# LSH attention and a gated feed-forward block on one core: query scale folded into the queries, negated maximum as bias, and another order on ScalarE in even slots

## The chip, the cores and the metric

The kernel runs on one core of one Trainium2 chip. The metric is device time in microseconds (us) of one execution. The kernel before takes 633.65 us (median of three runs, 633.51 to 634.42). A difference of 0.2%, some 1.3 us, is about what can be told from none.

The engines are named as in the profile: PE is TensorE's matmuls, PEld its weight loads, DVE is VectorE, ACT is ScalarE, POOL is GpSimd, SP issues DMAs.

## What is computed

There are 4 batches, 8 heads, 768 positions and a head size of 64. Every query and key gets a bucket of 6 sign bits, a query sees only the keys of its own bucket, and the attention's result goes through a gated feed-forward block:

```python
q_bits = (np.einsum('bhsd,dk->bhsk', q, proj) > 0)      # k_bits alike
mask = q_bucket[:, :, :, None] == k_bucket[:, :, None, :]
scores = (1 / np.sqrt(D)) * np.matmul(q, k.transpose(0, 1, 3, 2))
scores = np.where(mask, scores, -1000000000.0)
attn = np.exp(scores - np.max(scores, axis=-1, keepdims=True))
attn = attn / (np.sum(attn, axis=-1, keepdims=True) + 1e-09)
x = np.matmul(attn, v)                                  # heads side by side: B, S, 512
gate = sigmoid(causal 5-tap convolution of x along S, per channel)
out = (gate * (x @ w_val)) @ w_out
```

A query whose bucket holds no key has only masked scores, and its row of `attn` is then 1/768 everywhere. The factor 1/sqrt(D) is 1/8.

## The kernel before

A **unit** is one batch and head (32 of them), a **tile** is 128 queries of a unit against all its 768 keys (6 a unit, 192 in all). The main loop (L453) takes one **slot** k per tile. Every engine runs its instructions in the order in which the program writes them, so the order inside a slot is an order written out by hand.

The mask sits in the matmul: `prep` (L157) stacks, for the unit after the present one, the query rows and twelve rows of bits in `aq`, the key rows and bits in `ak`, and the parts lost by rounding in `bq` and `bk`. A bit that differs adds -2^60 to the score. GpSimd makes `aq` (L166) and `bq` (L168), and SP's DMAs copy the other halves (L169 to L175). `bits` (L186) makes the bit rows of four heads at a time from the raw tiles `r`. The first unit is stacked by `first_prep` (L205) on ACT, DVE and POOL.

What one slot k issues, in this order:

- ACT: `keep_transposed(k-4)`, two copies (L289) that empty the two PSUM banks `tp` into `pt`.
- DVE: `maxima(k)` (L238), the negated row maximum `nm` of the scores; in even slots `row_sums(k-2)` (L262) and `recip(k-2)` (L266) for the pair of tiles k-2 and k-1; `factors(k)` (L244), which is 1/8, or 0 where all scores of a row are masked; and `shifts(k)` (L248), `nm` times that factor.
- POOL: `normalise(k-2)` (L271), in place on `p`.
- PE: `scores(k+1)` (L232), four matmuls into a PSUM buffer `s`.
- ACT: `exponentials(k)` (L256), with `gs` as scale, `nb` as bias and the row sum as accumulator.
- `step(convs)` (in odd slots, from slot 60 on in all): one step of the convolution, on DVE (L323, L332, L334) and POOL (L324).
- Steps that round and split the feed-forward weights (first batch).
- PE and DVE: one step of `moe`, the feed-forward block of the batch before: four matmuls (L365 for the values, L390 for the output) with what follows them; three steps in two slots after the gates (L339, L481).
- `step(preps)`.
- In odd slots: two steps of `attn_v` (L303), two key blocks each; a unit's sixth step also issues the two **value copies** on ACT (L311) from PSUM `av` to `x`.
- PE: `transposes(k-3)` (L280), six matmuls, three into each of the two `tp` banks.

Buffers that matter here: `s` has 2, `tp` 2 (both used by one tile), `av` 1, and the pool of `p` is

```python
pp = ctx.enter_context(tc.tile_pool(name="pp", bufs=LAG + 1))     # line 55, LAG = 3
```

So tile k writes the `p` buffer that tile k-4 used, and its transposes need the banks that the copies of the tile before empty.

Of the kernel before, what the change touches and what calls it, by code (L numbers as in the profile page):

```python
# [19 lines left out]
BIG = float(2.0 ** 60)  # L20
# [6 lines left out]
def kernel(  # L27
# [10 lines left out]
    nc = tc.nc  # L38
    B, H, _, S = qk.shape
# [117 lines left out]
    def prep(i):  # L157

        if i >= len(units):
            return  # L160
        b, h = units[i]
        j = h % 4
        load_values(i)
        r = raws[i]
        aq, ak, bq, bk = stacks[i] = [stk.tile([P, S], FP32R, name=nm) for nm in ("aq", "ak", "bq", "bk")]
        nc.gpsimd.tensor_copy(out=aq, in_=r)  # L166
        yield
        nc.gpsimd.tensor_tensor(out=bq, in0=r, in1=aq.bitcast(FP32), op=ALU.subtract)  # L168
        nc.sync.dma_start(out=ak[0:D].bitcast(FP32), in_=aq[D:P].bitcast(FP32))  # L169
        nc.sync.dma_start(out=bk[0:D].bitcast(FP32), in_=aq[D:P].bitcast(FP32))  # L170
        nc.sync.dma_start(out=bk[D:P].bitcast(FP32), in_=bq[D:P].bitcast(FP32))
        nc.sync.dma_start(out=bq[D:P].bitcast(FP32), in_=aq[0:D].bitcast(FP32))
        u = cur["u"]
        nc.sync.dma_start(out=aq[D:M].bitcast(FP32), in_=u[32 * j:32 * j + 2 * NB].bitcast(FP32))
        nc.sync.dma_start(out=ak[D:M].bitcast(FP32), in_=u[32 * j + 2 * NB:32 * j + 4 * NB].bitcast(FP32))  # L175
        load_raw(i + 5)
        if j == 3 and i + 1 < len(units):
            yield
            yield from bits(i + 1)
# [25 lines left out]
    def first_prep():  # L205

        r = raws[0]
        aq, ak, bq, bk = stacks[0] = [stk.tile([P, S], FP32R, name=nm) for nm in ("aq", "ak", "bq", "bk")]
        z = ps_t.tile([P, 512], FP32, name="tp")
        for g in range(4):  # L210
            nc.tensor.matmul(out=z[32 * g:32 * g + 2 * NB, 0:HS], lhsT=proj_sb[:, 2 * NB * (g // 2):2 * NB * (g // 2 + 1)],
                             rhs=r[:, HS * (g % 2):HS * (g % 2 + 1)], start=True, stop=True, tile_position=(0, 32 * g))
        nc.scalar.copy(out=aq[0:D], in_=r[0:D])
        nc.vector.tensor_copy(out=bk[D:P], in_=r[D:P])
        nc.vector.tensor_copy(out=ak[0:D], in_=r[D:P])
        nc.gpsimd.tensor_tensor(out=bk[0:D], in0=r[D:P], in1=bk[D:P].bitcast(FP32), op=ALU.subtract)
        nc.vector.tensor_tensor(out=bq[D:P], in0=r[0:D], in1=aq[0:D].bitcast(FP32), op=ALU.subtract)
        for g in (0, 2, 3, 1):
            nc.vector.tensor_scalar(out=(aq, ak)[g // 2][D:M, HS * (g % 2):HS * (g % 2 + 1)],
                                    in0=z[32 * g:32 * g + 2 * NB, 0:HS],  # L220
                                    scalar1=rows_sb[32 * g:32 * g + 2 * NB, 2:3],
                                    scalar2=rows_sb[32 * g:32 * g + 2 * NB, 3:4], op0=ALU.is_ge, op1=ALU.mult)
        nc.scalar.copy(out=bq[0:D], in_=r[0:D])

    def scores(k):
        i, qt = tiles[k]
# [7 lines left out]

    def maxima(k):
        s = ss[k]
        nm = small.tile([P, 1], FP32, name="nm")
        nc.vector.tensor_reduce(out=nm, in_=s[:, :, 0:HS], axis=AX.XY, op=ALU.max, negate=True)  # L238
        nms[k] = nm

    def factors(k):

        gs[k] = small.tile([P, 1], FP32, name="gs")
        nc.vector.tensor_scalar(out=gs[k], in0=nms[k], scalar1=BIG / 2, scalar2=scale, op0=ALU.is_lt, op1=ALU.mult)  # L244

    def shifts(k):
        nbs[k] = small.tile([P, 1], FP32, name="nb")
        nc.vector.tensor_scalar(out=nbs[k], in0=nms.pop(k), scalar1=gs[k], scalar2=None, op0=ALU.mult)  # L248

    def exponentials(k):  # L250
        s, nb = ss.pop(k), nbs.pop(k)
        p = pp.tile([P, 2, HS], FP32, name="p")
        if k % 2 == 0:
            cur["sm"] = small.tile([P, 2, 2], FP32, name="sm")
        sm = cur["sm"]
        nc.scalar.activation(out=p, in_=s[:, :, 0:HS], func=AF.Exp, bias=nb, scale=gs.pop(k), accum_out=sm[:, k % 2, 0:1])  # L256
        ps[k] = (p.rearrange("p a b -> p (a b)"), sm)


    def row_sums(k):  # L260
        sums[k] = small.tile([P, 2, 2], FP32, name="s1")
        nc.vector.tensor_scalar(out=sums[k][:, :, 0], in0=ps[k][1][:, :, 0], scalar1=1e-9, scalar2=None, op0=ALU.add)  # L262

    def recip(k):
        ri = small.tile([P, 2], FP32, name="ri")
        nc.vector.reciprocal(out=ri, in_=sums.pop(k)[:, :, 0])  # L266
        rcs[k], rcs[k + 1] = ri[:, 0:1], ri[:, 1:2]

    def normalise(k):
        p, _ = ps[k]  # L270
        nc.gpsimd.tensor_scalar(out=p, in0=p, scalar1=rcs.pop(k), scalar2=1.0, op0=ALU.mult, op1=ALU.mult)  # L271

    def transposes(k):
        p, _ = ps.pop(k)
# [19 lines left out]
    def attn_v(i, pts):  # L294
        b, h = units[i]
        hh, c = h % 2, h // 2
        av = ps_v.tile([P, 512], FP32, name="av")
        vt = vts[i]
        for kb in range(KB):
            if kb:  # L300
                yield
            for s, pt in enumerate(pts):
                nc.tensor.matmul(out=av[s * D:(s + 1) * D, 0:HS], lhsT=vt[:, kb, hh * D:(hh + 1) * D], rhs=pt[kb // 3][:, kb % 3, :],  # L303
                                 start=(kb == 0), stop=(kb == KB - 1), tile_position=(0, s * D))
        if hh == 0:
            x = cur["x"] = xp.tile([P, S + KW - 1], FP32, name="x")
            nc.gpsimd.memset(x[:, 0:KW - 1], 0.0)
        x = cur["x"]
        for s in range(2):
            o = KW - 1 + s * HS  # L310
            nc.scalar.copy(out=x[hh * D:(hh + 1) * D, o:o + HS], in_=av[s * D:(s + 1) * D, 0:HS])  # L311
        if hh == 1:
            if c == 0:
                cur["xs"], cur["g"] = {}, []
            convs.append(pair_x(b, c, x, cur["g"], cur["xs"]))
# [105 lines left out]
    units = [(b, h) for b in range(B) for h in range(H)]  # L421
    tiles = [(i, qt) for i in range(len(units)) for qt in range(KB)]

    raws, stacks, vts, ss, nbs, ps, tps, sums, rcs, nms, gs, cur = {}, {}, {}, {}, {}, {}, {}, {}, {}, {}, {}, {}
    avs, convs, moes = [], [], []
    accs = [(ps_m, "m")]

    def step(gens):
# [13 lines left out]
    with tc.manual_schedule(engines=ENGINES):  # L442
        for i in range(5):
            load_raw(i)
        load_values(0)
        first_prep()
        weights = [[load_conv(), load_weights(0)], [load_weights(1)]]
        preps = [first_bits(), prep(1)]
        scores(0)
        step(weights[0])  # L450
        step(weights[1])
        turn = 0
        for k in range(N + LAG + 1):  # L453
            if 0 <= k - LAG - 1:
                keep_transposed(k - LAG - 1)
            pair = k % 2 == 0 and 0 <= k - 2 < N
            if k < N:
                maxima(k)
            if pair:
                row_sums(k - 2)  # L460
            if k < N:
                factors(k)
            if pair:
                recip(k - 2)
            if 0 <= k - 2 < N:
                normalise(k - 2)
            if k < N:
                shifts(k)
            if k + 1 < N:
                if tiles[k + 1][0] != tiles[k][0]:  # L470
                    finish(preps)
                    preps = [prep(tiles[k + 1][0] + 1)]
                scores(k + 1)
            if k < N:
                exponentials(k)
            if k >= 60 or k % 2:
                step(convs)
# [79 lines left out]
```

## Time and profile before

| | |
|---|---|
| median of the runs | 633.65 us |
| the profiled execution's span | 633.2 us |
| busy share of PE, PEld, DVE, ACT, POOL | 93%, 67%, 71%, 67%, 61% |
| mean granted TensorE clock | 0.986 |
| chain that ended last, by engine | PE 69%, ACT 14%, DVE 12%, issue 2%, DMA 2% |

How to read the views. The page gives each engine's busy time and the chain of waits. The view of the waits has, for each pair of lines, the time that the first sat idle for the second: "us in total, times, longest". The timeline has the start, the length, engine, line, operation, out<-in, shapes, how many were merged, and in brackets the idle time before it with what ended it. The groups by line give busy time, mean nanoseconds of one and the idle time ahead. The view by stage gives, for a stretch "from:to", its length, the busy time of each engine with the number of its instructions behind an x, then the granted clock, the DMA share and GB/s; for one line alone it shows that line's engines only. Matmuls overlap, so their lengths add up to more than the time they take; starts are compared instead.

### The profile page before, as it was taken

The page shows a single profiled execution, that of the slowest core. Times are in us where ns is not written, and L with a number is a line of the kernel's source. Part 1 is how long each engine was busy: PE and PEld are TensorE (multiplying, and loading weights), DVE is VectorE, ACT ScalarE, POOL GpSimd, SP SyncE. Part 2 cuts the span into 40 slices and gives each one's busy share as a digit, 9 for nine tenths or more (in the row PEclk, how much of TensorE's full clock was granted, in tenths as well). Part 3 has the DMA queues.
Part 4 walks back from the last instruction along what each step waited for, and adds up shares of the span by engine and source line. Part 5 has one row for each costly group of instructions (what it writes and reads, how often), then busy time and mean ns, then how long its engine had stood idle before and what let it go on. Part 6 is the DMA issues. An engine that isn't in the chain of part 4 may idle for free.

```text
span 633.2 us, 10639 instructions
## 1 busy us (share of the span) xinstructions
PE 591.4 (93%) x3496; PEld 426.2 (67%) x3496; DVE 451.3 (71%) x1033; ACT 421.1 (67%) x881; POOL 386.0 (61%) x357
## 2 busy tenths in 40 slices
PE   3699888989999999999999999999999999999997
PEld 2476555546667777676657777677667777776895
DVE  5689798999885856668675867668584786665532
ACT  3487777768778676667787776667778667675400
POOL 1476877778966765467754776467663677544221
PEclk9889997989999999999999999999999999999999
DMA  6533534443433334243333234243422223300111
GB/s 244 131 83 92 152 95 139 112 126 91 106 79 80 72 77 122 72 103 97 105 80 93 74 80 122 70 122 81 122 55 61 56 55 81 85 18 2 50 51 50
DMA packets 23270, 56.77 MB, mean 90 GB/s; under 512 B 4296, under 2 KB 4296, under 8 KB 23216
## 3 DMA queue, kind: packets, MB, share of 16 engines
q1 hardware_dynamic: 23072, 56.06, 33.3%
q8 instruction: 28, 0.46, 0.3%
q14 instruction: 26, 0.21, 0.1%
q10 hardware_dynamic: 144, 0.03, 0.0%
HBM read 23.12 MB, written 6.29 MB: 46 GB/s over the span
## 4 chain that ended last, share of the span: by engine, by line
PE 69%; ACT 14%; DVE 12%; issue 2%; DMA 2%; POOL 0%; SPq 0%; ACTq 0%; POOLq 0%; DVEq 0%
PE av L303 19%; PE s L232 17%; PE tp L280 12%; PE m L390 8%; PE m L365 7%; ACT p L256 6%; ACT pt L289 4%; DVE nm L238 3%; ACT x L311 3%; PE tp L365 1%; PE tp L390 1%; PE s L390 1%; DVE u L197 1%; PE tp L194 1%; DVE g L334 1%
## 5 line engine op out<-in xcount | busy, mean ns | idle before, releaser
L271 POOL TENSOR_SCALAR p<-p,ri 128x768 f32<-128x768 f32 x192 | 215.9, 1129 | 173.8 <-DVE nb L248 149.6
L238 DVE TENSOR_REDUCE nm<-s 128x1 f32<-128x768 f32 x192 | 182.5, 951 | 64.3 <-PE s L232 64.2
L289 ACT COPY pt<-tp 128x384 f32<-128x384 f32 x384 | 166.1, 485 | 86.7 <-PE tp L280 85.8
L256 ACT ACTIVATE p<-s,nb,gs 128x768 f32<-128x768 f32 x192 | 192.4, 1002 | 47.0 <-DVE nb L248 41.1
L280 PEld LDWEIGHTS tp<-ident,p 128*128 128x128 f32 x1152 | 131.2, 142 | 73.2 <-issue 46.4
L280 PE MATMUL tp<-ident,p 128*128 128x128 f32 x1152 | 166.3, 281 | 3.8 <-DVE u L197 1.5
L303 PE MATMUL av<-pt,vt 128*64 128x384 f32 x768 | 147.6, 506 | 0.0
L232 PE MATMUL s<-ak,aq 76*128 76x384 f32 x384 | 119.5, 393 | 28.9 <-ACT p L256 24.7
L232 PE MATMUL s<-bk,bq 128*128 128x384 f32 x384 | 101.6, 346 | 0.0
L303 PEld LDWEIGHTS av<-pt,vt 128*64 128x64 f32 x768 | 47.6, 137 | 63.7 <-issue 63.1
L232 PEld LDWEIGHTS s<-ak,aq 76*128 76x128 f32 x384 | 59.9, 196 | 45.2 <-ACT p L256 38.0
L334 DVE SCALAR_TENSOR_TENSOR g<-x,cw_sb,g 128x768 f32<-128x768 f32 x64 | 77.9, 1217 | 0.2
L232 PEld LDWEIGHTS s<-bk,bq 128*128 128x128 f32 x384 | 72.4, 195 | 0.5 <-issue 0.5
L376 POOL TENSOR_TENSOR hl<-ht,hh 128x384 fp32r<-128x384 f32 x32 | 32.2, 1006 | 45.9 <-DVE hh L374 45.9
L168 POOL TENSOR_TENSOR bq<-r,aq 128x768 fp32r<-128x768 f32 x31 | 58.3, 1882 | 0.0
L311 ACT COPY x<-av 64x384 f32<-64x384 f32 x64 | 30.3, 474 | 33.8 <-PE av L303 33.2
L365 PE MATMUL m<-xh,wv 128*128 128x384 f32 x200 | 42.8, 338 | 0.0
L248 DVE TENSOR_SCALAR nb<-nm,gs 128x1 f32<-128x1 f32 x192 | 39.9, 208 | 3.5
L324 POOL TENSOR_TENSOR xl<-x,xh 128x384 fp32r<-128x384 f32 x32 | 33.5, 1062 | 12.3 <-DVE xh L323 12.3
L370 DVE TENSOR_TENSOR ht<-m,g 128x384 f32<-128x384 f32 x25 | 13.9, 555 | 35.4 <-PE m L365 32.0
L256 ACT ACTIVATION_READ_ACCUMULATOR p<-s,nb,gs 128x1 f32 x192 | 39.0, 203 | 0.0
L390 PE MATMUL m<-wo,hh 128*128 128x512 f32 x144 | 38.2, 395 | 0.0
(84 smaller groups left out, 487.4 us busy)
## 6 DMA issues: line engine op xcount, KB each, us to landing
r<-in_qk_dram SPq DMA_DIRECT2D x32, 384.0 KB
vt<-in_v_dram SPq DMA_DIRECT2D x16, 384.0 KB
out_dram<-o SPq DMA_DIRECT2D x24, 256.0 KB
ak<-aq SPq DMA_DIRECT2D x31, 192.0 KB
bk<-aq SPq DMA_DIRECT2D x31, 192.0 KB
bk<-bq SPq DMA_DIRECT2D x31, 192.0 KB
bq<-aq SPq DMA_DIRECT2D x31, 192.0 KB
w<-in_w_val_dram SPq DMA_DIRECT2D x4, 512.0 KB
```

What stands on the lines that cost most here:

```text
L168: nc.gpsimd.tensor_tensor(out=bq, in0=r, in1=aq.bitcast(FP32), op=ALU.subtract)
L232: nc.tensor.matmul(out=s[:, hf, 0:HS], lhsT=lq[0:n, qs], rhs=rk[0:n, hf * HS:(hf + 1) * HS], start=n == M, stop=n == P)
L238: nc.vector.tensor_reduce(out=nm, in_=s[:, :, 0:HS], axis=AX.XY, op=ALU.max, negate=True)
L256: nc.scalar.activation(out=p, in_=s[:, :, 0:HS], func=AF.Exp, bias=nb, scale=gs.pop(k), accum_out=sm[:, k % 2, 0:1])
L271: nc.gpsimd.tensor_scalar(out=p, in0=p, scalar1=rcs.pop(k), scalar2=1.0, op0=ALU.mult, op1=ALU.mult)
L280: nc.tensor.transpose(out=tp[:, n * P:(n + 1) * P], in_=p[:, kb * P:(kb + 1) * P], identity=ident)
L289: nc.scalar.copy(out=pt[:, :, qo:qo + P], in_=tp[:, 0:HS].rearrange("p (a b) -> p a b", b=P))
L303: nc.tensor.matmul(out=av[s * D:(s + 1) * D, 0:HS], lhsT=vt[:, kb, hh * D:(hh + 1) * D], rhs=pt[kb // 3][:, kb % 3, :], start=(kb == 0), s ...
L311: nc.scalar.copy(out=x[hh * D:(hh + 1) * D, o:o + HS], in_=av[s * D:(s + 1) * D, 0:HS])
L334: nc.vector.scalar_tensor_tensor(out=g, in0=x[:, k:k + S], scalar=w, in1=g, op0=ALU.mult, op1=ALU.add)
L365: nc.tensor.matmul(out=acc[:, 0:HS], lhsT=wv[wi][:, c, j * P:(j + 1) * P], rhs=xs_[(c, o)][xi], start=(m == 0), stop=(m == 11))
L390: nc.tensor.matmul(out=acc, lhsT=hs[(o, j)][hi][:, tb * P:(tb + 1) * P], rhs=wo[wi][:, j, :], start=(m == 0), stop=(m == 11))
```

## The change

The diff does four things.

1. The factor 1/8 goes into the queries: for every unit but the first, VectorE multiplies the query half of the raw tile `r` in place, ahead of GpSimd's copy in `prep`; the first unit's copies become scaled copies. `factors` and `shifts` on DVE go, and the exponential has `nm` as its bias and no scale operand.
2. Rows with only masked scores are set right in the normalisation: `evens` makes 1/768 or 0 for a pair of tiles and `factors` turns the reciprocal of the sum into 0 there, so that `normalise` computes p * factor + even. Both work on the pair's two columns, once in two slots.
3. In even slots `exponentials(k)` stands ahead of `keep_transposed(k-4)` on ACT; odd slots keep their order.
4. The value copies are no longer issued with the last step of `attn_v` (odd slots) but in the next even slot, behind the copies of transposes.

The core of it:

```diff
@@ prep
+        nc.vector.tensor_scalar(out=r[0:D], in0=r[0:D], scalar1=scale, scalar2=None, op0=ALU.mult)
         nc.gpsimd.tensor_copy(out=aq, in_=r)
@@ first_prep
-        nc.scalar.copy(out=aq[0:D], in_=r[0:D])
+        nc.scalar.mul(out=aq[0:D], in_=r[0:D], mul=scale)
-        nc.vector.tensor_tensor(out=bq[D:P], in0=r[0:D], in1=aq[0:D].bitcast(FP32), op=ALU.subtract)
+        nc.vector.scalar_tensor_tensor(out=bq[D:P], in0=r[0:D], scalar=scale, in1=aq[0:D].bitcast(FP32),
+                                       op0=ALU.mult, op1=ALU.subtract)
-        nc.scalar.copy(out=bq[0:D], in_=r[0:D])
+        nc.scalar.mul(out=bq[0:D], in_=r[0:D], mul=scale)
@@ maxima, factors and shifts, exponentials
-        nm = small.tile([P, 1], FP32, name="nm")
-        nc.vector.tensor_reduce(out=nm, in_=s[:, :, 0:HS], axis=AX.XY, op=ALU.max, negate=True)
-        nc.vector.tensor_scalar(out=gs[k], in0=nms[k], scalar1=BIG / 2, scalar2=scale, op0=ALU.is_lt, op1=ALU.mult)
-        nc.vector.tensor_scalar(out=nbs[k], in0=nms.pop(k), scalar1=gs[k], scalar2=None, op0=ALU.mult)
+        if k % 2 == 0:
+            cur["nm"] = small.tile([P, 2], FP32, name="nm")
+        nms[k] = cur["nm"][:, k % 2:k % 2 + 1]
+        nc.vector.tensor_reduce(out=nms[k], in_=s[:, :, 0:HS], axis=AX.XY, op=ALU.max, negate=True)
+        if k % 2:
+            pairs[k - 1] = cur["nm"]
-        nc.scalar.activation(out=p, in_=s[:, :, 0:HS], func=AF.Exp, bias=nb, scale=gs.pop(k), accum_out=sm[:, k % 2, 0:1])
+        nc.scalar.activation(out=p, in_=s[:, :, 0:HS], func=AF.Exp, bias=nms.pop(k), accum_out=sm[:, k % 2, 0:1])
@@ evens, factors, normalise
+        nc.vector.tensor_scalar(out=even, in0=pairs[k], scalar1=BIG / 2, scalar2=1.0 / S, op0=ALU.is_ge, op1=ALU.mult)
+        nc.vector.scalar_tensor_tensor(out=ri, in0=pairs.pop(k), scalar=BIG / 2, in1=sums.pop(k + 1),
+                                       op0=ALU.is_lt, op1=ALU.mult)
-        nc.gpsimd.tensor_scalar(out=p, in0=p, scalar1=rcs.pop(k), scalar2=1.0, op0=ALU.mult, op1=ALU.mult)
+        nc.gpsimd.tensor_scalar(out=p, in0=p, scalar1=rcs.pop(k), scalar2=evs.pop(k), op0=ALU.mult, op1=ALU.add)
@@ attn_v
+        outs.append(lambda: values_out(b, hh, c, av))
+
+    def values_out(b, hh, c, av):
@@ the loop over slots
-            if 0 <= k - LAG - 1:
+            if 0 <= k - LAG - 1 and k % 2:
                 keep_transposed(k - LAG - 1)
...
             if pair:
                 row_sums(k - 2)
-            if k < N:
-                factors(k)
-            if pair:
+                evens(k - 2)
                 recip(k - 2)
+                factors(k - 2)
             if 0 <= k - 2 < N:
                 normalise(k - 2)
-            if k < N:
-                shifts(k)
...
             if k < N:
                 exponentials(k)
+            if k % 2 == 0:
+                if 0 <= k - LAG - 1:
+                    keep_transposed(k - LAG - 1)
+                while outs:
+                    outs.pop(0)()
             if k >= 60 or k % 2:
                 step(convs)
```

More of the change, by code (lines that the diff above doesn't have):

```diff
@@ L236, in maxima @@
         s = ss[k]
-        nm = small.tile([P, 1], FP32, name="nm")
[L238 to L248, printed above, removed]
+        if k % 2 == 0:
[4 more added lines that the diff above has]
+            pairs[k - 1] = cur["nm"]
     def exponentials(k):
-        s, nb = ss.pop(k), nbs.pop(k)
+        s = ss.pop(k)
         p = pp.tile([P, 2, HS], FP32, name="p")
@@ L255, in exponentials, with evens, factors @@
         sm = cur["sm"]
-        nc.scalar.activation(out=p, in_=s[:, :, 0:HS], func=AF.Exp, bias=nb, scale=gs.pop(k), accum_out=sm[:, k % 2, 0:1])
+        nc.scalar.activation(out=p, in_=s[:, :, 0:HS], func=AF.Exp, bias=nms.pop(k), accum_out=sm[:, k % 2, 0:1])
         ps[k] = (p.rearrange("p a b -> p (a b)"), sm)
     def row_sums(k):
-        sums[k] = small.tile([P, 2, 2], FP32, name="s1")
-        nc.vector.tensor_scalar(out=sums[k][:, :, 0], in0=ps[k][1][:, :, 0], scalar1=1e-9, scalar2=None, op0=ALU.add)
+        sums[k] = small.tile([P, 2], FP32, name="s1")
+        nc.vector.tensor_scalar(out=sums[k], in0=ps[k][1][:, :, 0], scalar1=1e-9, scalar2=None, op0=ALU.add)
+    def evens(k):
+        even = small.tile([P, 2], FP32, name="ev")
+        nc.vector.tensor_scalar(out=even, in0=pairs[k], scalar1=BIG / 2, scalar2=1.0 / S, op0=ALU.is_ge, op1=ALU.mult)
+        evs[k], evs[k + 1] = even[:, 0:1], even[:, 1:2]
     def recip(k):
+        r0 = sums[k + 1] = small.tile([P, 2], FP32, name="r0")
+        nc.vector.reciprocal(out=r0, in_=sums.pop(k))
+    def factors(k):
         ri = small.tile([P, 2], FP32, name="ri")
-        nc.vector.reciprocal(out=ri, in_=sums.pop(k)[:, :, 0])
+        nc.vector.scalar_tensor_tensor(out=ri, in0=pairs.pop(k), scalar=BIG / 2, in1=sums.pop(k + 1),
+                                       op0=ALU.is_lt, op1=ALU.mult)
         rcs[k], rcs[k + 1] = ri[:, 0:1], ri[:, 1:2]
@@ L422 @@
     tiles = [(i, qt) for i in range(len(units)) for qt in range(KB)]
-    raws, stacks, vts, ss, nbs, ps, tps, sums, rcs, nms, gs, cur = {}, {}, {}, {}, {}, {}, {}, {}, {}, {}, {}, {}
-    avs, convs, moes = [], [], []
+    raws, stacks, vts, ss, ps, tps, sums, rcs, evs, nms, pairs, cur = {}, {}, {}, {}, {}, {}, {}, {}, {}, {}, {}, {}
+    avs, outs, convs, moes = [], [], [], []
     accs = [(ps_m, "m")]
@@ L491 @@
         finish(avs)
+        while outs:
+            outs.pop(0)()
         cur["gates"] = 0
```

## The prediction, made before the result

> **What bounds the kernel now.** I read the page first, then the waits by engine, then the timeline of one stretch engine by engine, then the stages.
>
> ```profile
> span 633.2 us, 10639 instructions
> PE 591.4 (93%) x3496; PEld 426.2 (67%) x3496; DVE 451.3 (71%) x1033; ACT 421.1 (67%) x881; POOL 386.0 (61%) x357
> ```
>
> ```profile
> PE s L232 <- ACT p L256: 24.7, 40, 3.4
> ```
>
> TensorE is busy 93% of the span, and what it waits for is one thing: the scores (L232) wait 40 times, 24.7 us in all, for an exponential (L256) that must give a PSUM score buffer back. So I looked at what makes that exponential late. These are rows of the matmul timeline, then of ScalarE's, then of VectorE's, in a stretch without feed-forward work (start, length, what):
>
> ```profile
> 301.88 0.61 PE L232 MATMUL s<-ak,aq 76*128 76x384 f32 x2 [0.25 <-ACT p L256]
> ...
> 304.22 0.88 PE L280 MATMUL tp<-ident,p 128*128 128x128 f32 x6
> 304.85 0.60 PE L232 MATMUL s<-ak,aq 76*128 76x384 f32 x2
> ...
> 305.65 0.82 PE L280 MATMUL tp<-ident,p 128*128 128x128 f32 x6
> 306.70 0.62 PE L232 MATMUL s<-ak,aq 76*128 76x384 f32 x2 [0.23 <-ACT p L256]
> ...
> 309.04 0.87 PE L280 MATMUL tp<-ident,p 128*128 128x128 f32 x6
> ...
> 312.04 0.62 PE L232 MATMUL s<-ak,aq 76*128 76x384 f32 x2 [0.42 <-ACT p L256]
> ```
>
> ```profile
> 304.81 0.86 ACT L289 COPY pt<-tp 128x384 f32<-128x384 f32 x2 [1.21 <-PE tp L280]
> 305.55 1.01 ACT L256 ACTIVATE p<-s,nb,gs 128x768 f32<-128x768 f32 x1
> ...
> 306.53 0.87 ACT L289 COPY pt<-tp 128x384 f32<-128x384 f32 x2
> ...
> 309.15 0.97 ACT L311 COPY x<-av 64x384 f32<-64x384 f32 x2 [0.73 <-PE av L303]
> ```
>
> ```profile
> 302.89 0.96 DVE L238 TENSOR_REDUCE nm<-s 128x1 f32<-128x768 f32 x1 [0.47 <-PE s L232]
> ...
> 309.66 0.92 DVE L323 CAST xh<-x 128x384 fp32r<-128x384 f32 x2 [0.54 <-ACT x L311]
> 310.66 0.96 DVE L238 TENSOR_REDUCE nm<-s 128x1 f32<-128x768 f32 x1
> ```
>
> Call an even slot k. Its maximum is there at 303.85, but ScalarE idles 1.21 us, because first in its queue are the copies of the transposes of tile k-4, and those transposes start only at 304.22. The copies start at 304.81 (after the third transpose), the exponential at 305.55, and the scores of k+2 at 306.70. I measure everything from the first transpose of tile k-4: scores of k+2 come **2.48 us** later (306.70 - 304.22). Every third even slot has the value copies in front too, and there it is **3.00 us** (312.04 - 309.04).
>
> **What the new order makes of that ring.** The exponential may not simply start at 303.85. It writes a p buffer; line 55 gives LAG+1 = 4 of them, so tile k takes the one of tile k-4, whose last readers are the six transposes at 304.22 to 305.10. Today this wait is invisible, since the copies in front of the exponential wait for the same transposes, but for the third instead of the sixth. So the exponential gains only 305.55 - 305.14 = 0.41 us. The copies, now behind it, lose more; and the next transposes (tile k-3, same slot) need both of the two tp PSUM banks that these copies empty. The new ring from the first transpose:
>
> - 0.88 until the sixth transpose has ended (row 304.22), and 0.04 to the start that this allows (an estimate, at most the 0.14 by which the scores of 306.70 follow the exponential's end at 306.56);
> - 0.90 from the exponential's start to the next copy: 0.98 today (305.55 to 306.53), less one pointer operand;
> - 0.86 for the two copies, 0.03 release;
> - 0.32 for the three transposes into the second bank: six take 304.85 - 304.22 = 0.63;
> - then the scores of k+2. Sum **3.03 us**.
>
> The exponential's own saving has these rows:
>
> ```profile
> L256 ACT ACTIVATE p<-s,nb,gs 128x768 f32<-128x768 f32 x192 | 192.4, 1002 | 47.0 <-DVE nb L248 41.1 <-DVE cwt L92 4.1 <-PE tp L280 1.2
> ...
> L248 DVE TENSOR_SCALAR nb<-nm,gs 128x1 f32<-128x1 f32 x192 | 39.9, 208 | 3.5
> ...
> L244 DVE TENSOR_SCALAR gs<-nm 128x1 f32<-128x1 f32 x192 | 29.2, 152 | 3.3
> ...
> L338 ACT ACTIVATE g<-g 128x768 f32<-128x768 f32 x16 | 12.2, 832 | 0.0
> ```
>
> With two pointer operands it takes 1.00 us, the sigmoid of the same size with none 0.83. Dropping one of two lies between 0 and 0.17; I take half, 0.08. If it is 0, the ring is 3.11; if 0.17, 2.94.
>
> So each even slot costs the larger of 3.03 and what it has today. Where feed-forward matmuls stand between the scores and the transposes, today's figure is larger:
>
> ```profile
> 215.14 0.88 PE L280 MATMUL tp<-ident,p 128*128 128x128 f32 x6
> ...
> 217.82 0.59 PE L232 MATMUL s<-ak,aq 76*128 76x384 f32 x2
> ```
>
> ```profile
> 233.04 0.87 PE L280 MATMUL tp<-ident,p 128*128 128x128 f32 x6
> ...
> 235.95 0.59 PE L232 MATMUL s<-ak,aq 76*128 76x384 f32 x2
> ```
>
> That is 2.68 with a step of four value matmuls (L365) and 2.91 with one of four output matmuls (L390). The losses per even slot: plain 0.55, with value copies 0.03, with L365 0.35, with L390 0.12.
>
> **How many of each.** The views by stage, first of the maxima (L238), then of L365, then of L390; the number behind x counts instructions:
>
> ```profile
> 38.00:190.00 152.00, 52.39 (x56) 0.97 0.42 110
> 300.00:327.00 27.00, 9.56 (x10) 1.00 0.39 100
> 457.00:472.00 15.00, 5.29 (x6) 1.00 0.30 73
> ```
>
> ```profile
> 190.00:578.00 388.00, 120.83 (x127) 1.00 0.32 81
> ```
>
> ```profile
> 190.00:578.00 388.00, 60.96 (x286) 50.62 (x287) 1.00 0.32 81
> ```
>
> ```profile
> 190.00:578.00 388.00, 47.68 (x180) 33.31 (x180) 1.00 0.32 81
> ```
>
> Two slots are a pair. Without feed-forward work there are 28 pairs in the first batch (38 to 190 us) and 5 + 3 = 8 in two later gaps. The other 127 - 16 = 111 slots are 55 pairs with it, a third of them (18) with value copies. L365 has 286/4 = 71 steps, of which 12 share a slot with two others (the gates counter, lines 339 and 481: 3 batches, 2 slots, 2 extra steps), so 59 slots; L390 has 45. Half of each are even, two thirds of those without value copies: 20 and 15.
>
> - The 8 pairs: today a pair lasts 306.70 - 301.88 = 4.82, with value copies 5.34, mean 4.99; in the new order 4.82 + 0.55 = 5.37 for all. 8 x 0.38 = **+3.0**.
> - The 55 pairs: 20 x 0.35 + 15 x 0.12 + 18 x 0.03 = **+9.3**.
> - The 28 pairs of the first batch. Here VectorE is the other limit:
>
> ```profile
> 38.00:190.00 152.00, 137.88 (x830) 89.62 (x831) 134.53 (x300) 114.77 (x250) 117.39 (x104) 0.97 0.42 110
> ```
>
> A pair takes 152/28 = 5.43, that is 0.44 over the ring's 4.99, because VectorE (134.53/28 = 4.80 of work a pair) is 96% of that ring and its maxima come late. The change takes two gs and two nb off a pair (0.72) and puts two ops of two columns in (between 0.15 and 0.21 each, so 0.36), and a third of a query scaling (below, 0.2). VectorE is then at 4.64 of 5.37, 86%. The lateness falls to between 0 and 0.44; I take 0.2: 28 x (5.57 - 5.43) = **+4** (from -2 to +11).
>
> **The other edits.** The query scaling is a VectorE op ahead of GpSimd's copy of the same unit (31 times). A row of its kind stands alone at 0.61 and beside a GpSimd op at 1.75:
>
> ```profile
> 314.37 0.61 DVE L332 TENSOR_SCALAR g<-x,cw_sb 128x768 f32<-128x768 f32 x1
> ```
>
> ```profile
> 80.43 1.75 DVE L332 TENSOR_SCALAR g<-x,cw_sb 128x768 f32<-128x768 f32 x1
> ```
>
> I take 0.6, since GpSimd's next op, the copy, waits for it; behind that copy waits a normalisation whose factor VectorE makes later still, so the wait costs nothing there. The Trainium skill, "GPSIMD Engine Reference", section 1 Specifications, says that GpSimd shares its SBUF interfaces with VectorE and contends with 2-port ops: by it, and by the second row, the first batch would pay up to 9 x 1.15 = 10 us more VectorE time, which I keep for the upper end. The unit's DMAs on SP's queue start later by the same 0.6 us, for a unit that begins six slots (three pairs of some 5 us) later; only at the start is there no such cover:
>
> ```profile
> 20.31 0.67 DVE L197 TENSOR_SCALAR u<-m,packed 128x384 fp32r<-128x384 f32 x1
> ```
>
> ```profile
> 20.32 0.82 POOL L166 CAST aq<-r 128x768 fp32r<-128x768 f32 x1
> ```
>
> Unit 1's copy would start at 20.98 + 0.6 instead of 20.32, +1.26, less one gs and one nb (0.36) on the way there, and through GpSimd's subtraction and two DMAs it sets when tile 6 begins: **+0.7** (0 to 1.9). First-unit edits replace copies with scaled copies of the same size: 0. The normalisation gets a second pointer operand on GpSimd; even at the 0.17 above, 192 of them are 33 us of the 247 that GpSimd is idle: 0.
>
> The value copies move behind the copies of transposes. From slot 60 on, the split of x (L323) is queued in the same slot on VectorE, ahead of the odd slot's maximum. It would wait from 309.66 to about 312.7 (exponential 309.96, copies to 311.72, value copies 0.97), and the maximum after it moves from 310.66 to about 313.2. The following even slot's maximum can then be up to 1.0 late, or hidden. That is once in 12 slots, 11 times; I take 0.3: **+3** (0 to 11). The reductions of odd slots (gs, nb gone) shorten nothing that ends last.
>
> Sum: 3.0 + 9.3 + 4 + 0.7 + 3 = +20 on the span of 633.2; the median of the runs, 633.65, is 0.5 above the span: **653.5 us**. A difference of 0.2%, 1.3 us, is about what can be told from none.
>
> **Rivals.**
>
> *Faster: the exponential really goes early.* If it starts when its maximum is there, the only limit is TensorE's own order, and the 0.42 us between 306.28 (transposes from 305.65 on, 0.63) and 306.70 goes: 36 plain pairs x 0.42 = 15, so 619 us. For it speak the idle 1.21 us and the maximum at 303.85. It decides at one point: does the exponential of an even slot start before the sixth transpose of tile k-4 ends? Against it stands line 55. Chance, with all other ways to be faster, 0.13.
>
> *About the same.* VectorE's relief takes all lateness out of the first batch (-2), the start and the split of x cost nothing, and the 0.35 in feed-forward slots is an overestimate by half (+5), against +3 in the gaps: within some us. Inside 0.2%: chance 0.05.
>
> *Slower still.* The scaling is contended (+10) and the late maximum after the split of x costs its full 1.0 (+8): 672 us. Chance 0.10, counted as slower.
>
> The forecast's own case has 0.72. Its ends: ring 0.08 shorter or longer (it binds 59 pairs without value copies when shorter, all 91 when longer: -5, +7), lateness 0 to 0.44 (-6, +7), split of x at 0 or at 1.0 (-3, +8); not all fall to one side at once, so 638 to 668. The faster case lies below that and the two others mostly inside, so the range is **636 to 667**. Chances: faster 0.13, same 0.05, slower 0.82.
>
> **What would show it.** In the changed profile: plain even slots with the exponential starting 0.9 us after the first transpose of tile k-4 and lasting 0.92; a new TensorE wait, transposes (L280) for ScalarE's copies, of about 0.9 us, in place of the scores' wait for the exponential; 3.03 us from transposes to scores in all even slots but those with output matmuls; 5.4 us a pair from 300 to 327. If exponentials start ahead of the sixth transpose, or the waits of the scores are gone and nothing has replaced them, I am wrong. Wrong in size only: the lateness of the first batch.

## The result, and the profile after

The changed kernel takes 667.1 us (median of four runs, 666.2 to 668.7) against 633.6 us before (632.6 to 634.4): ratio **1.0533** (95% interval 1.0514 to 1.0552). The profiled execution has a span of 665.0 us against 633.2. It is slower, as forecast, and outside the first batch by the forecast mechanism, but by 33.5 us where 20 were forecast; 667.1 is just past the upper end of the range. Spans and stretches come from one execution of each kernel: that of before is about 1.5 us longer than its usual ones, so differences of spans from before are that much too small, and that of kfn_noscale, a version below, took 1947 us and is not read.

From line 166 on the line numbers of the code have moved: scores L234, maximum L242, exponential L252, transposes L287, copies of transposes L296, attn_v L310, value copies L321, split of x L333, convolution L342 and L344, query scaling L166.

The page of the changed kernel, then its view of the waits:

```profile
span 665.0 us, 10596 instructions
PE 599.8 (90%) x3496; PEld 420.8 (63%) x3496; DVE 454.0 (68%) x872; ACT 402.8 (61%) x881; POOL 404.3 (61%) x357
```

```profile
ACT p L252 <- PE tp L287: 107.3, 51, 3.7
...
PEld tp L287 <- issue: 83.3, 122, 2.8
...
DVE xh L333 <- ACT x L321: 40.3, 13, 6.2
...
PE tp L287 <- issue: 25.3, 28, 2.5
...
PEld av L310 <- ACT pt L296: 6.9, 19, 0.6
...
PE s L234 <- ACT p L252: 4.1, 9, 1.3
```

The time is waiting rather than work: against the page of before ScalarE works 18 us less, VectorE 3 and TensorE 8 more, and GpSimd 18 more, of which more below. The scores' wait for the exponential, 24.7 us before, is down to 4.1. In its place the exponential waits for transposes (107.3 us, 1.2 before) and the transposes wait (25.3 on the matmuls, which before waited 3.8 for everything together, and 83.3 on their weight loads, 46.4 before). From the views of before:

```profile
L280 PE MATMUL tp<-ident,p 128*128 128x128 f32 x1152 | 166.3, 281 | 3.8 <-DVE u L197 1.5 <-ACT pt L289 0.9 <-POOL p L271 0.6
```

```profile
PEld tp L280 <- issue: 46.4, 77, 1.2
```

The trace of the changed kernel puts these waits down to "issue", that is, to nothing it can name; the timeline of a plain even slot shows what they are. TensorE, then ScalarE:

```profile
321.89 0.88 PE L287 MATMUL tp<-ident,p 128*128 128x128 f32 x6
...
324.31 0.88 PE L287 MATMUL tp<-ident,p 128*128 128x128 f32 x6 [0.84 <-issue]
324.95 0.60 PE L234 MATMUL s<-ak,aq 76*128 76x384 f32 x2
...
327.28 0.87 PE L287 MATMUL tp<-ident,p 128*128 128x128 f32 x6
```

```profile
322.85 0.90 ACT L252 ACTIVATE p<-s,nm 128x768 f32<-128x768 f32 x1 [1.61 <-PE tp L287]
323.65 0.19 ACT L252 ACTIVATION_READ_ACCUMULATOR p<-s,nm 128x1 f32 x1
323.75 0.85 ACT L296 COPY pt<-tp 128x384 f32<-128x384 f32 x2
```

The transposes of tile k-4 run from 321.89 to 322.77; the exponential of k starts at 322.85, 0.96 after the first of them; the copies follow at 323.75; the transposes of k-3 start at 324.31, while the second copy still runs (to 324.60); the scores of k+2 come at 324.95. That is a ring of **3.06 us** (forecast 3.03). Two slots last 327.28 - 321.89 = 5.39 us (forecast 5.37). This slot is no exception: from slot 68 on every even slot has a ring of 3.06 to 3.36, but for six of 4.41 to 4.75.

### The profile page after: what moved, and what is told of

Same layout as the page of the kernel before. It is cut to its first block, busy times and chain, and to the rows that moved or that the text cites. A ratio compares the mean times of both kernels' runs of the same rounds, so it can differ in the third digit from the quotient of the medians.

```text
span 665.0 us, 10596 instructions
## 1 busy us (share of the span) xinstructions
PE 599.8 (90%) x3496; PEld 420.8 (63%) x3496; DVE 454.0 (68%) x872; ACT 402.8 (61%) x881; POOL 404.3 (61%) x357
## 4 chain that ended last, share of the span: by engine, by line
PE 70%; DVE 13%; ACT 7%; issue 5%; POOL 3%; DMA 1%; ACTq 0%; POOLq 0%; DVEq 0%
PE tp L287 18%; PE av L310 16%; PE s L234 16%; PE m L400 8%; PE m L375 6%; DVE nm L242 4%; ACT p L252 3%; ACT pt L296 1%; POOL p L278 1%; PE tp L375 1%; PE tp L400 1%; PE s L400 1%; ACT x L321 1%; PE m L195 1%; DVE xh L333 1%
## 5 line engine op out<-in xcount | busy, mean ns | idle before, releaser
L278 POOL TENSOR_SCALAR p<-p,ri,ev 128x768 f32<-128x768 f32 x192 | 230.6, 1204 | 149.1 <-DVE ri L272 87.3
L252 ACT ACTIVATE p<-s,nm 128x768 f32<-128x768 f32 x192 | 174.3, 908 | 188.2 <-PE tp L287 107.3
L242 DVE TENSOR_REDUCE nm<-s 128x1 f32<-128x768 f32 x192 | 181.4, 949 | 60.3 <-PE s L234 59.9
L287 PE MATMUL tp<-ident,p 128*128 128x128 f32 x1152 | 170.8, 284 | 42.8 <-issue 25.3
L287 PEld LDWEIGHTS tp<-ident,p 128*128 128x128 f32 x1152 | 123.9, 142 | 134.5 <-issue 83.3
L296 ACT COPY pt<-tp 128x384 f32<-128x384 f32 x384 | 166.3, 483 | 23.2 <-PE tp L287 22.6
L310 PE MATMUL av<-pt,vt 128*64 128x384 f32 x768 | 150.9, 505 | 0.3 <-ACT x L321 0.3
L234 PE MATMUL s<-ak,aq 76*128 76x384 f32 x384 | 118.0, 388 | 11.3 <-ACT p L252 4.1
L234 PE MATMUL s<-bk,bq 128*128 128x384 f32 x384 | 101.7, 346 | 0.2 <-POOL aq L167 0.2
L310 PEld LDWEIGHTS av<-pt,vt 128*64 128x64 f32 x768 | 50.8, 137 | 64.4 <-issue 54.1
L344 DVE SCALAR_TENSOR_TENSOR g<-x,cw_sb,g 128x768 f32<-128x768 f32 x64 | 80.8, 1263 | 0.2
L234 PEld LDWEIGHTS s<-bk,bq 128*128 128x128 f32 x384 | 72.2, 195 | 0.7 <-POOL aq L167 0.7
L234 PEld LDWEIGHTS s<-ak,aq 76*128 76x128 f32 x384 | 59.7, 196 | 18.4 <-ACT p L252 8.1
L169 POOL TENSOR_TENSOR bq<-r,aq 128x768 fp32r<-128x768 f32 x31 | 63.4, 2045 | 0.0
L386 POOL TENSOR_TENSOR hl<-ht,hh 128x384 fp32r<-128x384 f32 x32 | 33.4, 1044 | 34.7 <-DVE hh L384 33.6
L333 DVE CAST xh<-x 128x384 fp32r<-128x384 f32 x32 | 21.5, 681 | 42.0 <-ACT x L321 40.3
L167 POOL CAST aq<-r 128x768 fp32r<-128x768 f32 x31 | 25.7, 828 | 25.6 <-PE tp L287 12.3
L252 ACT ACTIVATION_READ_ACCUMULATOR p<-s,nm 128x1 f32 x192 | 38.2, 199 | 0.0
```

What stands on the lines that cost most here:

```text
L234: nc.tensor.matmul(out=s[:, hf, 0:HS], lhsT=lq[0:n, qs], rhs=rk[0:n, hf * HS:(hf + 1) * HS], start=n == M, stop=n == P)
L242: nc.vector.tensor_reduce(out=nms[k], in_=s[:, :, 0:HS], axis=AX.XY, op=ALU.max, negate=True)
L287: nc.tensor.transpose(out=tp[:, n * P:(n + 1) * P], in_=p[:, kb * P:(kb + 1) * P], identity=ident)
L296: nc.scalar.copy(out=pt[:, :, qo:qo + P], in_=tp[:, 0:HS].rearrange("p (a b) -> p a b", b=P))
L344: nc.vector.scalar_tensor_tensor(out=g, in0=x[:, k:k + S], scalar=w, in1=g, op0=ALU.mult, op1=ALU.add)
L386: nc.gpsimd.tensor_tensor(out=hl, in0=ht, in1=hh.bitcast(FP32), op=ALU.subtract)
```

## Where the time went, by stretch

The experiments below are read by stretches. Each is the time between the first scores matmul of two tiles in the profiled execution: from tile 8 to 66 is the first batch without feed-forward work; "feed-forward" is 66 to 94, 112 to 146 and 160 to 188; "gaps" is 94 to 112 and 146 to 160. The names of the versions are explained with the experiments.

| version | median, us | ratio to before (interval) | span | to tile 8 | first batch | feed-forward | gaps | after 188 |
|---|---|---|---|---|---|---|---|---|
| before | 633.6 | 1 | 633.2 | 34.0 | 156.7 | 284.7 | 86.1 | 71.8 |
| after | 667.1 | 1.0533 (1.0514-1.0552) | 665.0 | 34.4 | 169.1 | 294.8 | 94.1 | 72.6 |
| order_only | 689.6 | 1.0898 (1.0867-1.0930) | 684.8 | 35.0 | 169.9 | 305.8 | 100.6 | 73.5 |
| keep_first | 637.0 | 1.0057 (1.0035-1.0080) | 635.3 | 33.4 | 159.9 | 283.2 | 86.7 | 72.1 |
| keep_first_noval | 635.2 | 1.0021 (1.0010-1.0031) | 633.8 | 34.0 | 160.0 | 283.0 | 85.1 | 71.7 |
| novalmove | 663.9 | 1.0479 (1.0456-1.0502) | 663.9 | 33.9 | 169.9 | 295.2 | 92.9 | 72.0 |
| noscale | 662.0 | 1.0451 (1.0429-1.0473) | 659.6 | 33.8 | 164.0 | 294.8 | 94.3 | 72.7 |
| p5 | 644.2 | 1.0163 (1.0141-1.0185) | 642.3 | 34.1 | 168.3 | 283.0 | 85.1 | 71.7 |
| p5_noval | 651.4 | 1.0278 (1.0257-1.0300) | 651.1 | 34.0 | 170.0 | 287.9 | 87.2 | 71.9 |
| p5_late | 645.6 | 1.0184 (1.0167-1.0202) | 642.7 | 33.6 | 162.5 | 287.6 | 87.1 | 71.9 |
| p5_late_vm | 639.8 | 1.0094 (1.0066-1.0121) | 636.8 | 33.5 | 163.0 | 285.2 | 83.5 | 71.5 |
| before_p5 | 636.8 | 1.0049 (1.0034-1.0064) | 634.5 | 33.8 | 158.2 | 284.7 | 86.1 | 71.7 |
| kfn_act | **630.7** | **0.9953** (0.9936-0.9969) | 629.5 | 34.8 | 154.3 | 283.6 | 85.0 | 71.8 |
| kfn_noscale | 630.6 | 0.9951 (0.9934-0.9968) | | | | | | |

The 31.8 us of span are 12.5 in the first batch, 10.1 in the feed-forward stretches, 8.1 in the gaps, 0.4 at the start and 0.8 at the end (rounded). The prediction had 4 for the first batch.

## Experiments

The theory after the result: the ring through the p buffer costs what was forecast, and the first batch costs more because VectorE did not get earlier. Rivals: the waits of VectorE and GpSimd that the new factors and the query scaling bring are the real cost (A), or the moved value copies are (B).

**1. The order against the rest.** keep_first is the changed kernel with the copies ahead of the exponential again in even slots (the value copies stay in the even slot, behind the exponential):

```diff
-            if 0 <= k - LAG - 1 and k % 2:
+            if 0 <= k - LAG - 1:
                 keep_transposed(k - LAG - 1)
...
             if k % 2 == 0:
-                if 0 <= k - LAG - 1:
-                    keep_transposed(k - LAG - 1)
                 while outs:
```

> The changed kernel with one part undone: in even slots the copies of transposes stand ahead of the exponential again; the value copies stay in the even slot, now behind the exponential, and the scaled queries stay. Theory (the order makes the ring of 3.06 us, since the exponential waits for the sixth transpose of tile k-4): the exponential follows the copies, so the scores of k+2 come 2.40 us after the first transpose (2.48 before, less 0.09 for the shorter exponential), with the value copies behind it in every even slot, not 3.00 in every third; about 620 to 628 us. Rival A (the scaling on VectorE and its lateness cost the time): stays above 655 us. Rival B (the moved value copies cost it): 650 to 660 us.

order_only is the kernel before with the same lines in their changed form and the moved value copies, scale and factors as before.

> The kernel before with only the order changed: exponential ahead of the copies of transposes in even slots, value copies behind them; factor and shift stay on VectorE, the exponential keeps its scale operand. Theory: ring of 3.06 + 0.09 = 3.15 us after the first transpose in every even slot, plain pairs 5.47 us; 665 to 676 us. Rivals A and B' (scaling, or the new normalisation, cost the time): near 634 us.

Undoing the order takes the loss from 33.5 us to 3.6, so the order is the cause and rival A falls; but what is left does not gain, and the theory's 620 to 628 was wrong. Doing the order alone costs 56 us, more than all four parts together, and 14 above the theory's upper end. Its timeline shows what was left out of that sum. VectorE, then ScalarE, of order_only:

```profile
336.32 1.66 DVE L326 CAST xh<-x 128x384 fp32r<-128x384 f32 x2 [3.25 <-ACT x L314]
337.90 0.94 DVE L238 TENSOR_REDUCE nm<-s 128x1 f32<-128x768 f32 x1
...
339.20 0.95 DVE L238 TENSOR_REDUCE nm<-s 128x1 f32<-128x768 f32 x1
340.50 0.17 DVE L262 TENSOR_SCALAR s<-sm 128x2 f32<-128x2 f32 x1 [0.35 <-ACT p L256]
340.57 0.15 DVE L244 TENSOR_SCALAR gs<-nm 128x1 f32<-128x1 f32 x1
340.77 0.17 DVE L266 RECIPROCAL ri<-s 128x2 f32<-128x2 f32 x1
340.85 0.20 DVE L248 TENSOR_SCALAR nb<-nm,gs 128x1 f32<-128x1 f32 x1
```

```profile
339.38 0.99 ACT L256 ACTIVATE p<-s,nb,gs 128x768 f32<-128x768 f32 x1 [1.70 <-DVE nb L248]
...
341.16 0.99 ACT L256 ACTIVATE p<-s,nb,gs 128x768 f32<-128x768 f32 x1 [0.70 <-PE s L232]
```

The split of x waits 3.25 us for the value copies, the odd slot's maximum stands behind it, and that exponential starts at 339.38. The even slot's maximum is there at 340.15, but gs and nb stand behind the row sums, which need the odd exponential: 340.50, 340.57, 340.85, exponential 341.16, a whole us after its maximum. (The bracket names the scores for this wait, but the scores of this tile had ended before its maximum began. The end of nb, 341.05, is 0.11 ahead of the exponential, as 339.28 is 0.10 ahead of 339.38. Likewise, where brackets below name the row sums, L257, the maximum ended about 0.1 before.) With the bias straight from the maximum this chain is gone. So parts 1 and 2 of the change make the new order some 20 us cheaper than it is alone.

**2. The p buffer.** p5 gives the pool a fifth buffer (and takes one from `u`, for room); before_p5 does that to the kernel before.

```diff
-    pp = ctx.enter_context(tc.tile_pool(name="pp", bufs=LAG + 1))
+    pp = ctx.enter_context(tc.tile_pool(name="pp", bufs=LAG + 2))
...
-        u = stk.tile([P, S], FP32R, name="u", bufs=2)
+        u = stk.tile([P, S], FP32R, name="u", bufs=1)
```

> The changed kernel with a fifth p buffer, so that the exponential of tile k need not wait for the transposes of tile k-4 (room for it by one buffer less for the bit rows u). Theory: the exponential of an even slot starts when its maximum is there, up to 0.4 us before the first transpose of tile k-4; the copies then start after the third transpose as before the change (0.59), and TensorE is the limit: scores of k+2 2.06 us after the first transpose, plain pairs 4.4 us; 615 to 632 us. Rivals (scaling or value copies): above 655 us.

> The kernel before with five p buffers and one u buffer fewer, as in the versions with the fifth buffer; nothing else changed. Theory (in the kernel before no instruction of the chain waits for a p buffer, since the exponential stands behind copies that come later than the buffer): 632.5 to 635 us. Rival A (a p buffer gains by itself, so what the versions with five buffers won proves nothing on the order): under 631.5 us. Rival B (the single u buffer delays the first batch by 2 us or more): 635.5 to 638 us.

ScalarE and TensorE of p5, a plain even slot:

```profile
313.84 0.90 ACT L252 ACTIVATE p<-s,nm 128x768 f32<-128x768 f32 x1 [0.33 <-DVE s L257]
314.64 0.19 ACT L252 ACTIVATION_READ_ACCUMULATOR p<-s,nm 128x1 f32 x1
314.73 0.85 ACT L296 COPY pt<-tp 128x384 f32<-128x384 f32 x2
```

```profile
314.12 0.88 PE L287 MATMUL tp<-ident,p 128*128 128x128 f32 x6
...
315.54 0.82 PE L287 MATMUL tp<-ident,p 128*128 128x128 f32 x6
316.12 0.59 PE L234 MATMUL s<-ak,aq 76*128 76x384 f32 x2
...
318.44 0.88 PE L287 MATMUL tp<-ident,p 128*128 128x128 f32 x6
```

Now the exponential starts 0.28 us ahead of the first transpose, the ring is 2.00 and two slots last 4.32: TensorE runs without a gap. All that the change lost in the feed-forward stretches and gaps is back (283.0 and 85.1), so there the p buffer is the cause. The first batch is hardly touched: 168.3 against 169.1. The theory's 615 to 632 fails by that. before_p5 is 3.5 us slower than before, near rival B: by the stretches 1.5 us of that lie in the first batch (158.2), and where the rest lies the two executions do not show. That burden is in every version with five buffers, so in the first batch the fifth buffer by itself may be worth some 2 us.

**3. What loses the first batch: the order again, behind late maxima.** p5_late has five p buffers and the value copies at their old place, and the new order only from slot 66 on; p5_noval is the same with the new order throughout.

```diff
-            if 0 <= k - LAG - 1 and k % 2:
+            if 0 <= k - LAG - 1 and (k % 2 or k < 66):
...
-                if 0 <= k - LAG - 1:
+                if 0 <= k - LAG - 1 and k >= 66:
```

> The changed kernel with a fifth p buffer (and one u buffer fewer, for room), and the value copies at their old place. Theory (the first batch is lost because copies behind the exponential now wait for late maxima, whatever becomes of the value copies): 641 to 645 us, first batch 165 to 168.5 us. Rival (with the p buffer free, it is the value copies ahead of the odd slot's copies that lose the first batch): 632 to 637 us, first batch 157 to 160 us.

> As the kernel with the fifth p buffer and the value copies at their old place, but in the slots below 66 (the first batch) the copies stand ahead of the exponential as before; from slot 66 on the exponential stands first. Theory (late maxima reach the copies only where these stand behind the exponential): first batch 158 to 160.5 us, the stretches after it as with the fifth buffer, 632 to 635.5 us in all. Rival (the first batch is lost to the scaling, the small instructions and GpSimd themselves, not to the order): first batch 165 us or more, 640 to 644 us in all.

Both are slower than either side expected, 651.4 and 645.6; most of what both have too much lies from slot 66 on and is the matter of point 5. Between the two it is nearly all the first batch that differs: 170.0 with the new order, 162.5 with the old (158 to 160.5 expected). The granted clock of that stretch was 0.94 in p5_noval and 0.99 in p5_late, but p5_late_vm below, with the old order there and 0.96, has 163.0, so the clock does not make the difference. So most of the first batch's loss is the order too, and a free buffer does not bring it back. The ring of 3.06 holds in slots 6n+4 (3.06 on average, 2.58 before); slots 6n have 3.71 (3.12 before), and with the fifth buffer even 4.48. It is in slots 6n that VectorE has the most ahead of the maximum. VectorE, GpSimd, ScalarE and TensorE of the changed kernel around tile 36:

```profile
113.84 1.24 DVE L92 TENSOR_SCALAR o<-o 128x512 f32<-128x512 f32 x1 [0.65 <-ACT o L90]
115.12 1.10 DVE L93 TENSOR_SCALAR o<-o 128x512 int32<-128x512 int32 x1
116.14 1.38 DVE L166 TENSOR_SCALAR r<-r 64x768 f32<-64x768 f32 x1
117.45 0.94 DVE L242 TENSOR_REDUCE nm<-s 128x1 f32<-128x768 f32 x1
...
120.28 2.28 DVE L342 TENSOR_SCALAR g<-x,cw_sb 128x768 f32<-128x768 f32 x1
```

```profile
115.90 1.20 POOL L112 TENSOR_TENSOR wo<-w 128x512 fp32r<-128x512 f32 x1
...
120.31 1.82 POOL L169 TENSOR_TENSOR bq<-r,aq 128x768 fp32r<-128x768 f32 x1
```

```profile
118.50 0.90 ACT L252 ACTIVATE p<-s,nm 128x768 f32<-128x768 f32 x1 [3.05 <-DVE s L257]
119.30 0.19 ACT L252 ACTIVATION_READ_ACCUMULATOR p<-s,nm 128x1 f32 x1
119.39 0.85 ACT L296 COPY pt<-tp 128x384 f32<-128x384 f32 x2
```

```profile
115.91 0.88 PE L287 MATMUL tp<-ident,p 128*128 128x128 f32 x6
...
119.96 0.89 PE L287 MATMUL tp<-ident,p 128*128 128x128 f32 x6 [2.47 <-issue]
120.60 0.83 PE L234 MATMUL s<-ak,aq 76*128 76x384 f32 x2
```

The maximum starts only after the query scaling, at 117.45; the exponential comes at 118.50, and now the copies wait behind it, so the transposes of k-3 stand 2.47 us and the ring is 4.70. In noscale (next point) this slot has 3.15. In the old order the copies need no maximum, so the transposes go on and only the scores of k+2 wait.

**4. The query scaling.** noscale leaves out the scaling on VectorE (and with it the factor 1/8 for all units but the first) from the changed kernel; keep_first_noval is parts 1 and 2 of the change alone, order and value copies as before; kfn_noscale and kfn_act are keep_first_noval without the scaling (again the factor 1/8 is left out) and with the scaling on ScalarE.

```diff
-        nc.vector.tensor_scalar(out=r[0:D], in0=r[0:D], scalar1=scale, scalar2=None, op0=ALU.mult)
+        nc.scalar.mul(out=r[0:D], in_=r[0:D], mul=scale)
```

> The changed kernel without the scaling of the queries on VectorE; it leaves out the factor 1/8 for all units but the first. Theory: the ring stays 3.06 us; only the lateness in every sixth slot of the first batch and 0.4 us at the start go: 659 to 664 us. Rival A (the scaling costs the time): 635 to 648 us.

> Scaled queries and negated maximum as bias alone: the order of exponential and copies and the place of the value copies are those of before. Theory (the scaling on VectorE costs the first batch some 3 to 5 us, which the two small instructions fewer in each slot do not quite repay; the value copies in the even slot cost 1 to 2 us through late x): 632 to 636 us, first batch 158 to 160 us, the stretches after it within 0.4 us of those of before. Rival A (the shorter way from maximum to exponential is worth what it looks like, and only the moved value copies hid it): 627 to 631 us.

> Scaled queries and negated maximum alone (order and place of all copies as before), without the instruction on VectorE that scales the queries of the units after the first: it leaves out the factor 1/8 for them. Theory (the first batch's 160.0 us of the kernel with the scaling, against 156.65 us before, are the scaling's): first batch 156 to 157.5 us, 630.5 to 632.5 us in all. Rival (they are the slower convolution and small instructions on VectorE, which share it with GpSimd's work otherwise than before): first batch 159 to 160.5 us, 633.5 to 635.5 us in all.

> Scaled queries and negated maximum alone (order and place of all copies as before), with the queries scaled by ScalarE instead of VectorE. Theory (ScalarE idles for over a third of the span, VectorE is what is late in the first batch): first batch 156 to 158.5 us, 630.5 to 633.5 us in all, the first version at or under the time before. Rival (31 instructions of some 0.9 us on ScalarE stand ahead of the copies of transposes once a unit): 635 to 640 us, with late transposes once in six slots over the whole span.

All four times came as the theory said. Without the scaling the changed kernel gains 5.1 us, all of it in the first batch (169.1 to 164.0); parts 1 and 2 alone go from 635.2 to 630.7 when ScalarE does it, again in the first batch (160.0 to 154.3, below the 156 expected). The stretches after it are 1.6 and 1.0 us shorter than before in keep_first_noval, more than the 0.4 expected. kfn_noscale says the same by its times. kfn_act leaves nothing out and beats both kernels, by 0.47% against before (0.31 to 0.64). ScalarE's 31 scalings, by group:

```profile
L166 ACT ACTIVATE r<-r 64x768 f32<-64x768 f32 x31 | 25.9, 836 | 0.0
```

That is more work than VectorE's (619 ns mean in the changed kernel), on the engine that has room.

**5. The value copies.** novalmove is the changed kernel with the value copies back in the odd slot; p5_late_vm is p5_late with the value copies moved from slot 66 on.

```diff
-        outs.append(lambda: values_out(b, hh, c, av))
+        values_out(b, hh, c, av)
```

> The changed kernel with the value copies back at the end of the attn_v work of the odd slot, exponential first in even slots and scaled queries kept. Theory (the order of exponential and copies carries nearly all of the loss; the moved value copies only add some waits of the first attn_v matmuls for copies, about ten times 0.31 us, and some late x): 660 to 665 us, and the slots k%6 == 4 without FFN work go back to 2.32 us from scores to first transpose. Rival A (the moved value copies are what spoils the first batch): 653 to 658 us, first batch 158 to 161 us instead of 169.1. Rival B (the value copies in the old place are as much in the way as in the new one): 666 to 669 us.

> Fifth p buffer; in the slots below 66 copies and value copies as before, from slot 66 on exponential first and value copies behind it. Theory (in the version with the value copies at their old place, every even slot of number 6n+2 had its exponential behind a value copy that waits for the last attn_v matmuls, so that it began 1.1 us after the first transpose and not 0.3 us before it): the stretches from slot 66 on as with the fifth buffer and moved value copies, 439.8 us up to the end instead of 446.7, 636 to 638.5 us in all. Rival (the place of the value copies makes no difference there, the 7 us have another cause): 643 to 646 us.

With four p buffers the move costs about 1 us (spans 663.9 and 665.0) to 3 (medians), as its theory said, and the first batch doesn't care (169.9): rival B falls. With five it is the other way round: p5_noval is 7.2 us slower than p5, and p5_late_vm 5.8 faster than p5_late. ScalarE and TensorE of p5_noval show why:

```profile
322.51 0.97 ACT L321 COPY x<-av 64x384 f32<-64x384 f32 x2 [0.73 <-PE av L310]
323.51 0.90 ACT L252 ACTIVATE p<-s,nm 128x768 f32<-128x768 f32 x1
```

```profile
322.40 0.88 PE L287 MATMUL tp<-ident,p 128*128 128x128 f32 x6
```

At their old place the value copies wait for the last attn_v matmul, and the exponential behind them comes 1.1 us after the first transpose instead of 0.28 before it. From slot 66 on p5_late_vm takes 440.2 us, as expected; its median is 1.3 us above the range expected, with 163.0 us in the first batch where p5_late had 162.5.

## Why the prediction was right in direction and too small

**The ring was right.** The p buffer holds the exponential to the sixth transpose, 0.96 us instead of 0.92 after the first; the ring is 3.06 (3.03), two plain slots 5.39 (5.37). p5 takes the buffer away as a limit and the whole loss of the later stretches goes with it.

**The exponential** takes 908 ns, not 1002: dropping one pointer operand is worth 0.094, where I took 0.08.

```profile
L252 ACT ACTIVATE p<-s,nm 128x768 f32<-128x768 f32 x192 | 174.3, 908 | 188.2 <-PE tp L287 107.3 <-DVE nm L242 28.6 <-DVE s L257 25.4
```

The Trainium skill, "ScalarE: Activation LUTs", section What ACT_TABLE_LOAD costs, states some 93 ns for each such operand; the trace agrees.

**The step that failed** is "The lateness falls to between 0 and 0.44; I take 0.2", with the 4.64 us of VectorE work a pair on which it stood. The views by stage of the 28 pairs from tile 10 to tile 66, before and after:

```profile
38.10:190.70 152.60, 138.34 (x833) 89.84 (x833) 135.13 (x301) 115.37 (x250) 117.99 (x104) 0.97 0.41 110
```

```profile
38.90:203.50 164.60, 137.62 (x835) 87.33 (x834) 140.79 (x253) 110.36 (x250) 119.16 (x104) 0.98 0.39 101
```

VectorE has 48 instructions fewer and works 5.7 us more: 5.03 us a pair instead of 4.83. A pair takes 5.88, which is 0.49 over the ring's 5.39, against 0.46 over 4.99 before: the lateness did not fall at all, and the 28 pairs cost 12.0 us, not 4. By spans the forecast is 11.8 us too low, and 8 of these are this term. The groups of the first batch, the convolution before and after, then the scaling, and the other versions say where the forecast relief went:

```profile
L334 DVE SCALAR_TENSOR_TENSOR g<-x,cw_sb,g 128x768 f32<-128x768 f32 x16 | 18.8, 1176 | 0.0
```

```profile
L344 DVE SCALAR_TENSOR_TENSOR g<-x,cw_sb,g 128x768 f32<-128x768 f32 x16 | 24.3, 1517 | 0.0
...
L166 DVE TENSOR_SCALAR r<-r 64x768 f32<-64x768 f32 x9 | 6.6, 729 | 0.0
```

The largest part is the query scaling. Its work is 6.6 us, near the 5.6 of the forecast (0.2 a pair), but it was priced as a share of VectorE's work, and it stands right ahead of the late maxima. Three versions with the new order price it: order_only has 169.9 us in the first batch; noscale, with the new factors and bias but no scaling, 164.0; the changed kernel 169.1. So the relief was there, 5.9 us (28 x 0.24 = 6.7 were forecast, the scaling included), and the scaling took 5.1 of it back.

The saving itself was also counted too high. The 0.72 a pair for two gs and two nb adds up lengths that overlap those of their neighbours (above, 340.57 + 0.15, 340.77 + 0.17 and 340.85 + 0.20); in the trace of before these instructions cover only 0.44 us a pair that no other VectorE instruction covers.

The convolution, which the change doesn't touch, takes 5.5 us longer for the same 16 instructions; 16.8 us of it lie beside GpSimd instructions, 12.9 before. That was in no term. Why is not settled: it is so in noscale (23.1 us) and kfn_act (21.5) too, but not in order_only (18.3), so it comes with the new factors, bias and normalisation. In kfn_act the span is nevertheless shorter. The second pointer operand of the normalisation, put at nothing, lengthens it from 1129 to 1204 ns, 14.7 us of GpSimd's work in all (1166 ns in kfn_act); what that costs in time is not shown.

Counted from before in another order, the new factors and bias gain 2.3 us in the first batch (156.7 before, 154.3 in kfn_act), the scaling on VectorE costs 5.7 (160.0 in keep_first_noval), and the order with the moved value copies 9.1 (169.1), where the ring's 0.38 a pair made 10.6. If the 1.5 us by which the execution of before is long lie in the first batch, the first of these is under 1 us; the scaling costs 5 to 6 us either way.

**Feed-forward stretches and gaps.** They lose 18.2 us where 15.3 were forecast with the split of x. The first attn_v matmuls of a unit now wait for copies of transposes that stand behind the value copies (the waits have 6.9 us in 19 such waits of weight loads); I had not seen that wait, and novalmove prices it, with what else the move does, at 1 to 3 us. The split of x waits 40.3 us for the value copies (10.0 before), but little of that ends last: the rings behind it are 3.06 to 3.36, up to 0.3 over the others and some 1.6 us in all, where 3 were forecast. **The start** is 0.4 us longer, where 0.7 were forecast; the versions that scale on VectorE have 33.4 to 34.4, so no cost is shown. (The terms of the prediction add up to 653.65, not 653.5.)

**The rivals.** "The exponential really goes early" was right on its decisive point, line 55: p5 is that case, though at 644.2 us and not 619, since the first batch keeps its loss. "Slower still" named contended scaling; 2 of the 9 scalings of the first batch were (1.38 us), the others took 0.54.

## What to carry to other kernels

Before moving an instruction forward in a queue, list all it waits for: here the buffer it writes was free later than its input was there, and every instruction that it passed then waited too. Price an added instruction by what waits behind it and not by its share of the engine's work: right ahead of late maxima, 6.6 us of scaling cost 5.1 us of time, and on ScalarE, which had room, nothing that shows. Two edits can have opposite signs alone and together (the moved value copies cost 1 to 3 us with four buffers and gain 6 to 7 with five), so test them in pairs.

## What the runs showed of the hardware

Where certain instructions of VectorE and GpSimd meet, one is held until the other is done, not slowed in proportion. The scaling that takes 0.54 us alone began at 116.14, GpSimd's instruction ended at 117.10, and the scaling took 1.38 = 0.96 + 0.42; the convolution's first step, 0.61 alone, took 2.28 and ended 0.43 after GpSimd's subtraction of 120.31 to 122.13. It is not always VectorE that is held:

```profile
301.59 1.78 DVE L344 SCALAR_TENSOR_TENSOR g<-x,cw_sb,g 128x768 f32<-128x768 f32 x1
303.29 0.54 DVE L166 TENSOR_SCALAR r<-r 64x768 f32<-64x768 f32 x1
```

```profile
301.54 1.01 POOL L386 TENSOR_TENSOR hl<-ht,hh 128x384 fp32r<-128x384 f32 x1
302.54 2.08 POOL L278 TENSOR_SCALAR p<-p,ri,ev 128x768 f32<-128x768 f32 x1
```

Here the convolution step, 1.00 to 1.01 alone, takes 1.78 and ends 0.82 after the first GpSimd instruction; the normalisation, 1.20 on average, then takes 2.08, and the scaling keeps its 0.54. The Trainium skill, "SBUF — State Buffer", section SBUF: two separate sides, describes a shared port pair locked for the whole instruction, on which the loser blocks; the trace agrees. The maximum, which reads PSUM, took 0.94 to 0.96 us throughout.
